# Attention and linear attention on one core: idle matmuls ahead of the second scores, projections planned by their users, products that wait for V's copies

## The chip, the cores and the metric

The kernel runs on one core of one Trainium2 chip. The metric is the device time of one execution in microseconds (us). The core has a matrix engine (PE, whose weight loads are listed apart as PEld), a vector engine (DVE), a scalar engine (ACT), a general engine (POOL), and queues of DMA that are fed by SP and ACT. Each engine works through its own instructions in the order in which the program lists them; semaphores make one wait for another.

## The reference

Two layers on separate inputs of 2048 rows by 512 columns, bf16, 32 heads of 16; their outputs lie side by side.

```python
# layer A: softmax attention
qkv = (x @ wqkv).reshape(B, S, 3, H, Dh)          # S = 2048, H = 32, Dh = 16
p = softmax(einsum("bhqd,bhkd->bhqk", q, k) * Dh ** -0.5)
a = einsum("bhqk,bhkd->bhqd", p, v).reshape(B, S, D) @ wo
# layer B: linear attention with learned feature maps
phi = concat(softmax(x_head @ w_phi), softmax(-(x_head @ w_phi)))   # for q and for k
o = (phi_q @ (phi_k.T @ v)) / (phi_q @ sum(phi_k) + 1e-6)
b = o.reshape(B, S, D) @ wo
return concat([a, b], axis=-1)
```

## The kernel before

**Layer A.** The 32 heads are eight groups of four; the four heads of a group lie in the four 32-row strips of the PE array. A unit is one group and one chunk of 512 queries: 32 units, chunk by chunk, group by group. A unit has 32 steps. One step (L986) computes the scores of two heads, 128 queries by 512 keys, into two PSUM banks with two matmuls on 32 rows each; the two pairs of banks 0 to 3 alternate between steps. DVE then takes the maximum of each row (L1000, 1024 steps in all). After the last step of a segment (a part of a unit: units 0 and 31 have three segments, the others two) DVE folds the maxima (L1010), POOL splits them in two bf16 parts (L1016 to L1019), and SP transposes them (L1021) and writes them into spare rows of QT (L1023). The scores are then computed a second time, transposed and with the maximum subtracted by those rows ("blocks", L1055), ACT takes the exponential (L1062) into a ring of 15 tiles, and "products" (L1108) multiply four such tiles by V, with a column of ones for the sums, into bank 7. Blocks of a segment begin `LAGX` = 8 steps after its last step. Behind a unit ACT copies bank 7 out (X), POOL takes reciprocals and multiplies (L1243), and the output projection of layer A follows by chunks.

**Projections.** `proj(kind, a, c)` makes a job of four matmuls and a copy. For groups 0 and 1 the copy goes straight into QT or KT (ACT, L530 and L532). Groups 2 to 7 are projected in pairs, eight heads at a time: ACT copies into `oct_t`, and two DMAs on SP (L519) spread it over two groups of QT or KT. V's jobs (L491) are copied into VP, one for each of 16 tiles of 128 keys.

**Layer B** runs in the same program as jobs in the background: weights are folded with the feature maps (`fold_job`), and 32 feature-map chains `fm(n)` open at step `FM0 + FMSTEP * n`.

**The planner.** The order of instructions on every engine is fixed when the program is built, by a loop that keeps an account (`_Clock`): `ck.pe` and `ck.rows` say where PE stands, `ck.act` where ACT stands, `ck.d[s]` when step s's maximum is done. Its figures: 1.131 for a step, 0.215 for a matmul, 0.445 from issue to result, 0.477 for an exponential. `tau` is the number of the next step. A job carries a step at which it opens (`slot`), a step at which it is due (`by`), and sometimes a condition (`when`). Once a job is due it goes ahead of the scores; else it is placed only where it fits ahead of the next ones. `XA` holds the account's times at which the four chunks of x may be used. `qt_ready`, `kt_ready` and `vp_ready` say that a projection has been issued; `ready_at` says at what time of the account its result is there, and the scores (`m1_from`) wait for it. `ready_at` is set for groups 0 and 1 only.

Among the fillers, `row_fill` (L1192) and `go_fill` (L1207) place matmuls on zeros where PE would rest, from step `LAG` = 22 on (14 steps of the first segment plus 8). Eleven such matmuls (L562) open the program, ahead of the first two projections.

Group 2's jobs open at steps 36, 42, 48, 54 (keys) and 60 (queries), each due ten steps later:

```python
        at = 36
        for g in range(2, NG, 2):
            for t in group(g):
                add_job(at, *proj(*t), by=at + 10)
                at += 6
```

`group(g)` lists four chunks of keys and then the queries of chunk 0. Unit 2 (group 2, chunk 0) begins at step 64, unit 4 at step 128, unit 6 at step 192.

Of the kernel before, what the change touches and what calls it, by code (L numbers as in the profile page):

```python
# [152 lines left out]
def bass_concat_heads__softmax_full_mha__linear_kernel_hedgehog__prompt_kernel(  # L153
# [9 lines left out]
    NKC = S // 512  # L163
# [16 lines left out]
    COLD = 7.0  # L180
    WARM = 7.4
    TOP = 12.0
    FM0 = 152
    FMSTEP = 25
    units = [(g, c) for c in range(NQC) for g in range(NG)]

    segs = []
# [22 lines left out]
    LAG = seg_end[0] + LAGX  # L210

    with contextlib.ExitStack() as es:
# [165 lines left out]
        def add_job(slot, pieces, fin, by=None, when=None, bank=None):  # L378
            by = slot + BY if by is None else by
            njobs[0] += 1  # L380
            jobs.append((by, slot, njobs[0], pieces, fin, when, bank))
# [106 lines left out]
        def proj(kind, a, c):  # L488
            if kind == "v":
                kt = a  # L490
                pieces = mm_pieces(lambda e, b, ct: e.matmul(  # L491
                    PS[:, b, :], xAT[:, ct, kt * 128:(kt + 1) * 128], wA[:, ct, 1024:1536],
                    start=(ct == 0), stop=(ct == 3)), [t_xa[kt // 4], t_wa[1024]])

                def fin(b, tok, tau):
                    last_proj["v"] = tok
                    vp_ready[kt] = aevac(VP[:, kt, :, 0:16], PS[:, b, :].rearrange("p (h d) -> p h d", d=16),
                                         [tok, t_vp1])
                    return vp_ready[kt]
                return pieces, fin  # L500
            g = a
            wpad = WQp if kind == "q" else WKp
            at = g if g < 2 else 1 + g // 2
            pieces = mm_pieces(lambda e, b, ct: e.matmul(  # L504
                PS[:, b, :], wpad[:, ct, 128 * at:128 * at + 128], xAT[:, ct, c * 512:(c + 1) * 512],
                start=(ct == 0), stop=(ct == 3)),
                [t_xa[c], (t_wqp if g < 2 else t_wqr) if kind == "q" else (t_wkp if g < 2 else t_wkr)])

            def fin(b, tok, tau):
                last_proj[kind] = tok  # L510
                sl = slice(c * 512, (c + 1) * 512)
                if g >= 2:

                    i = n_oct[0] % 2
                    n_oct[0] += 1
                    t = aevac(oct_t[:, i, :], PS[:, b, :], [tok, oct_d.get(i)])
                    dst, dep = (QT, t_qt0) if kind == "q" else (KT, t_kt1)
                    for gg in range(2):
                        oct_d[i] = P.dma("sp", d_oct[i], lambda e, gg=gg: e.dma_start(  # L519
                            dst[0:128:2, g + gg, sl], oct_t[64 * gg:64 * gg + 64, i, :]), [t, dep[g]])  # L520
                    for gg in range(2):
                        (qt_ready if kind == "q" else kt_ready)[(g + gg, c)] = oct_d[i]
                    return t
                if kind == "q" and g == 0 and c == 0:
                    t = P.op("dve", lambda e: e.tensor_copy(QT[:, g, sl], PS[:, b, :]), [tok])
                elif g == 0 and c == 0:
                    t = P.op("dve", lambda e: e.tensor_scalar(
                        KT[:, g, sl], PS[:, b, :], bias_k[:, 0:1], None, ALU.add), [tok, t_bias])
                elif kind == "q":
                    t = aevac(QT[:, g, sl], PS[:, b, :], [tok])  # L530
                else:
                    t = act_op(0.57, lambda e: e.activation(  # L532
                        KT[:, g, sl], PS[:, b, :], ACT.Identity, bias=bias_k[:, 0:1]), [tok, t_bias])
                (qt_ready if kind == "q" else kt_ready)[(g, c)] = t
                ready_at[(kind, g, c)] = ck.act + 0.25
                return t
            return pieces, fin

        def group(g):
            return [("k", g, c) for c in range(NKC)] + [("q", g, 0)]  # L540


        XA = (6.0, 11.9, 14.2, 18.8)
        need = [(4, "k", 0, 1), (6, "k", 0, 2), (8, "k", 0, 3)]
        need += [(LAG + 2 + kt, "v", kt, 0) for kt in range(NKT)]
        need += [(32 + 2 * c, "k", 1, c) for c in range(NKC)] + [(31, "q", 1, 0)]
        for at, t in enumerate(sorted(need)):
            c = t[2] // 4 if t[1] == "v" else t[3]
            add_job(at, *proj(*t[1:]), by=t[0] - 4, when=lambda c=c, v=t[1] == "v": ck.pe > max(XA[c], 11.8 * v))
        at = 36  # L550
        for g in range(2, NG, 2):
            for t in group(g):
                add_job(at, *proj(*t), by=at + 10)
                at += 6
        at = 170
        for c in range(1, NQC):
            for g in (0, 1, 2, 4, 6):
# [61 lines left out]
        def fold_job(x, ct):  # L619
            piece = mm_piece(4, cols=128, fn=lambda e, b, t: e.matmul(  # L620
                PS[:, b, t * 128:(t + 1) * 128], wT[4 * x + t][:, ct * 128:(ct + 1) * 128], BD[:, t, :],
                start=True, stop=True), deps=lambda: [BL["wt"], BL["bd"]])

            def fin(b, tok, tau):
                wf_pe[(x, ct)] = tok
                wf_tok[(x, ct)] = aevac(Wf[:, x, ct, :], PS[:, b, :], [tok, last_proj["k"]])
                return wf_tok[(x, ct)]
            return [piece], fin

        for i in range(8):  # L630
            add_job(125 + 3 * i, *fold_job(1 - i // 4, i % 4), by=130 + 3 * i)

        kv_last = {}

# [435 lines left out]
        def pv_at():  # L1070
            n = npv[0]
            if n == len(of_pv) or nblk[0] < min(pv_blk[0] + BATCH, len(of_b)):
                return None
            v = of_pv[n]
            per = 4 // segs[v][2]
            if any((n - seg_pv[v]) * per + j not in vp_ready for j in range(per)):
                return None
            at = max(exp_end[B] for B in range(pv_blk[0], min(pv_blk[0] + BATCH, len(of_b))))
            if n == seg_pv[v] and segs[v][1] == 0 and v > 0:
                if segs[v][0] - 1 not in xev_end:  # L1080
                    return None
                at = max(at, xev_end[segs[v][0] - 1])
            return ck.full("col", at)
# [117 lines left out]
        def go_fill():  # L1201
# [4 lines left out]
            for cq in range(4):  # L1206
# [3 lines left out]
                    skip_group_check=(bank == 7)),  # L1210
                    [t_zmv, t_ones, dep] if cq == 0 else [], signal=False)

        def emit_xev(u):
            ub = u % 2
            deps = [pv_t[u]]
            if u >= 1:
                deps.append(mul_t[u - 1])
            xev_t[u] = aevac(X[:, :], PVB, deps)
            xev_end[u] = ck.act + 0.18

            pv_open[0] = True
            pv_free[:] = [xev_end[u], xev_t[u]]
            lr_t[u] = P.dma("sp", d_lr[ub], lambda e: e.dma_start(lr[:, ub, :], X[16:128:32, :]),
                            [xev_t[u], lb_t.get(u - 2)])
# [90 lines left out]
        def step(tau):  # L1315
# [14 lines left out]
            for v in rm_in_slot.get(tau, []):  # L1330
                emit_mchain(v)
                ck.extra += 0.11

        tau = 0
        while tau < total_q1 or npv[0] < len(of_pv) or jobs or running or calls:
            bg_read(tau, ck.act + 0.05 if nblk[0] else 1e9)
# [29 lines left out]
            if due - HARD < first < 1e8 and tau < total_q1 and (second is None or second > first - 0.25):  # L1366
                step(tau)
                tau += 1
                if tau > LAG:
                    row_fill(tau)  # L1370
            elif cold and ck.full("col", fill_place()[1]) < min(soon, pick[0] if pick else 1e9) + 0.1:
                go_fill()
            elif pick is not None and pick[0] <= soon + 0.02:
                if pick[1] == 1 and not in_hand():
                    ck.begun = tau
                pick[2](tau)
            elif (tau >= LAG and ck.work(ck.pe) < WARM
                  and ck.full("col", fill_place()[1]) + 0.213 <= min(soon, pick[0] if pick else 1e9)):
                go_fill()
            elif pick is not None and pick[0] < soon + 0.1 and pick[1] == 0:  # L1380
                pick[2](tau)
            elif second is not None and second <= first + 0.05 and not (first <= feed and first < second):
                block_go(tau)
                if tau >= LAG:
                    row_fill(tau)
            elif running and not running[0][0] and running[0][4] <= first + 0.1:
                bg_read(tau, 1e9)
            elif first > 1e8:
                ck.pe = max(ck.pe + 0.2, max(ck.rows))
            else:  # L1390
                step(tau)
                tau += 1
                if tau > LAG:
                    row_fill(tau)
# [55 lines left out]
```

## Time and profile before

| | |
|---|---|
| median of 3 runs | 1264.46 us (1263.28 to 1265.48) |
| profiled execution | 1259.73 us, its span 1257.9 us |
| busy in the span | PE 1171.4, PEld 470.0, DVE 1205.4, ACT 1161.9, POOL 631.8 us |
| DVE L1000, maxima | 1024 instructions, 1171.7 us busy, 13.2 us idle before them |
| ACT L1062, exponentials | 2048 instructions, 1057.8 us busy, 62.6 us idle before them |
| first maximum starts, last folding of maxima | 10.27 us, 1222.87 us |
| chain that ended last | ACT 44%, DVE 30%, PE 21% of the span |

Times within the profile are microseconds from the start of the span. A line of the timeline gives start, length (of the merged run of instructions), engine, source line, operation, output and input, and the count; in brackets stands how long the engine was idle before it and what it then waited for. "PEclk" and "granted clock" are the PE clock as a share of full speed.

### The profile page before, as it was taken

The numbers are of one execution on the slowest core, as the hardware profiler recorded it, in microseconds if no ns is written. First come the engines' busy times: TensorE is split into PE (matmuls) and PEld (weight loads), VectorE is DVE, ScalarE is ACT, GpSimd is POOL, SyncE is SP. The second block draws the span as 40 slices with busy tenths as digits, with TensorE's granted clock in tenths as the row PEclk, the third lists the DMA queues.
The fourth block names the chain that finished last, engine by engine and source line by source line (L and its number), as shares of the span: only waits on it lengthen the run. The fifth ranks groups of instructions, "written<-read, shape, count | busy, mean of one in ns | idle before, by whom it ended". The sixth has DMA issues, their size and how long they took to land.

```text
span 1257.9 us, 37296 instructions
## 1 busy us (share of the span) xinstructions
PE 1171.4 (93%) x16122; PEld 470.0 (37%) x16230; DVE 1205.4 (96%) x1229; ACT 1161.9 (92%) x2296; POOL 631.8 (50%) x724
## 2 busy tenths in 40 slices
PE   7989999999999999999999999999999999999998
PEld 2333343333333333333333334333333333333334
DVE  6989999999999999999999999999999999999980
ACT  2788999999999899999999899999999999999997
POOL 3301111363558266666558355556757555658520
PEclk8999999999999999999999999999999999999999
DMA  6123411011100111011001112212121112121211
GB/s 134 38 49 67 63 12 9 5 12 12 13 7 13 21 13 12 7 14 13 9 8 9 26 9 25 30 16 38 17 33 18 43 24 34 9 37 21 35 17 28
DMA packets 84253, 31.46 MB, mean 25 GB/s; under 512 B 71864, under 2 KB 82104, under 8 KB 84088
## 3 DMA queue, kind: packets, MB, share of 16 engines
q1 hardware_dynamic: 82216, 28.02, 15.7%
q8 instruction: 127, 2.08, 0.7%
q10 hardware_dynamic: 1872, 1.05, 0.3%
q14 instruction: 38, 0.31, 0.1%
HBM read 3.16 MB, written 4.19 MB: 6 GB/s over the span
## 4 chain that ended last, share of the span: by engine, by line
ACT 44%; DVE 30%; PE 21%; POOL 2%; issue 2%; DMA 1%; ACTq 0%; SPq 0%
ACT pT L1062 39%; DVE part L1000 28%; PE PS L1055 5%; PE PS L986 4%; PE PS L504 2%; PE PS L1207 2%; PE PS L1108 2%; PE PS L1192 2%; ACT eB L696 1%; PE PS L491 1%; POOL den_t L856 1%; PE PS L650 1%; PE PS L880 1%; ACT oct_t L464 1%; ACT X L464 1%
## 5 line engine op out<-in xcount | busy, mean ns | idle before, releaser
L1000 DVE TENSOR_REDUCE part<-PS 128x2 f32<-128x1024 f32 x1024 | 1171.7, 1218 | 13.2 <-PE PS L1192 5.5
L1062 ACT ACTIVATE pT<-PS 128x512 bf16<-128x512 f32 x2048 | 1057.8, 639 | 62.6 <-PE PS L986 23.7
L1055 PE MATMUL PS<-QT,KT 32*128 32x256 bf16 (+1 forms) x4224 | 669.1, 269 | 21.6 <-ACT pT L1062 2.7
L1192 PE MATMUL PS<-zmv,ones_t 32*128 32x512 bf16 x1755 | 589.5, 383 | 0.1
L986 PE MATMUL PS<-KT,QT 32*128 32x512 bf16 x2048 | 447.3, 385 | 19.9 <-DVE part L1000 11.4
L1055 PEld LDWEIGHTS PS<-QT,KT 32*128 32x128 bf16 x4224 | 228.8, 92 | 368.1 <-ACT pT L1062 217.2
L1016 POOL TENSOR_SCALAR stage<-mrow 128x8 bf16<-128x8 f32 (+1 forms) x66 | 15.7, 238 | 406.0 <-DVE mrow L1010 406.0
L1108 PE MATMUL PS<-pT,VP 128*17 128x256 bf16 (+1 forms) x4224 | 203.3, 272 | 10.5 <-ACT pT L1062 1.6
L986 PEld LDWEIGHTS PS<-KT,QT 32*128 32x128 bf16 x2048 | 116.2, 91 | 115.0 <-DVE part L1000 73.8
L1192 PEld LDWEIGHTS PS<-zmv,ones_t 32*128 32x128 bf16 x1755 | 146.5, 91 | 1.4 <-PE PS L1055 0.7
L1207 PE MATMUL PS<-zmv,ones_t 128*17 128x256 bf16 x2880 | 141.4, 276 | 1.4
L1108 PEld LDWEIGHTS PS<-pT,VP 128*17 128x17 bf16 x4224 | 61.5, 88 | 120.0 <-ACT pT L1062 57.4
L1228 POOL TENSOR_TENSOR lr<-lr,neg 128x16 f32<-128x16 f32 x31 | 90.6, 2922 | 22.9 <-DMA lr<-X 11.9
L1243 POOL TENSOR_TENSOR QT<-X,Yd 128x256 bf16<-128x256 f32 x62 | 43.8, 727 | 91.0 <-DMA Yd<-Yd 91.0
L856 POOL TENSOR_TENSOR den_t<-den_t,neg 128x32 f32<-128x32 f32 x16 | 87.1, 5446 | 1.3
L727 POOL TENSOR_TENSOR wB<-wB,neg 128x32 f32<-128x32 f32 x16 | 87.0, 5437 | 0.0
L1207 PEld LDWEIGHTS PS<-zmv,ones_t 128*17 128x17 bf16 x2880 | 55.6, 89 | 75.0 <-issue 66.0
L747 POOL TENSOR_TENSOR wA<-eB,rB 128x512 bf16<-128x512 bf16 x64 | 66.9, 1069 | 0.2
L688 POOL TENSOR_TENSOR uB<-pB,mB 128x512 f32<-128x512 bf16 x32 | 33.6, 1049 | 33.0 <-DVE mB L672 33.0
L704 POOL TENSOR_TENSOR sB<-eB 128x512 f32<-128x512 bf16 x32 | 36.9, 1154 | 5.2 <-ACT eB L696 5.2
L707 POOL TENSOR_TENSOR sB<-sB 128x256 f32<-128x256 f32 x64 | 36.2, 566 | 5.0
L650 PE MATMUL PS<-WKp,xBT 128*128 128x512 bf16 x99 | 31.2, 383 | 7.3 <-ACT pT L1062 6.1
(90 smaller groups left out, 568.1 us busy)
## 6 DMA issues: line engine op xcount, KB each, us to landing
Yd<-Yd SPq DMA_DIRECT2D x124, 32.0 KB, 3.2
out_dram<-xAT SPq DMA_DIRECT2D x16, 128.0 KB, 1.8
KT<-oct_t SPq DMA_DIRECT2D x24, 64.0 KB, 2.1
QT<-oct_t SPq DMA_DIRECT2D x24, 64.0 KB, 2.0
out_dram<-OA SPq DMA_DIRECT2D x12, 128.0 KB, 1.7
mcols<-stage SPq DMA_TRANSPOSE x66, 2.2
QT<-mcols SPq DMA_DIRECT2D x62, 4.0 KB
wA<-in_A_wqkv_dram SPq DMA_DIRECT2D x2, 384.0 KB, 4.6
```

The source lines that it names most:

```text
L727: t = P.op("pool", lambda e: e.tensor_tensor(wB[:, n % 4, :], wB[:, n % 4, :], neg1[:, 0:1].broadcast_to([128, 32]), ALU.pow), [cx["r"], t ...
L747: t = P.op("pool", lambda e, a=a: e.tensor_tensor(f4[:, :, a, :], e4[:, :, a, :], r2[:, :, 1 - a].unsqueeze(2).broadcast_to([128, H, 16]), ...
L856: cx["rd"] = P.op("pool", lambda e: e.tensor_tensor(den_t[:, :], den_t[:, :], neg1[:, 0:1].broadcast_to([128, 32]), ALU.pow), [t, t_neg])
L986: tok = P.op("pe", lambda e, r=r, bank=2 * (q1 % 2) + i: e.matmul(PS[:, bank, :], QT[32 * r:32 * r + 32, g, q0:q0 + 128], KT[32 * r:32 * r ...
L1000: r1[q1] = P.op("dve", lambda e: e.tensor_reduce(part[:, u % 2, 2 * pr:2 * pr + 2, qt, kc], PS[:, b:b + 2, :], AX.X, ALU.max), deps)
L1055: m2_t[B] = P.op("pe", lambda e, j=j: e.matmul(PS[:, bank, j * w:j * w + w], KT[32 * r:32 * r + 32, g, (kt + j) * 128:(kt + j + 1) * 128], ...
L1062: exp_t[B] = P.op("act", lambda e: e.activation(pT[:, slot, :], PS[:, bank, :], ACT.Exp, scale=0.25), [m2_t[B], slot_reader.get(slot)])
L1108: tok = P.op("pe", lambda e, B=B, r=r, j=j: e.matmul(PVB[32 * r:32 * r + 17, lo:lo + w], VP[:, kt + j, 4 * g + r, :], pT[:, B % RING, j * ...
L1192: fill_tok[0] = P.op("pe", lambda e: e.matmul(PS[:, 7, :], ones_t[32 * r:32 * r + 32, :], zmv[32 * r:32 * r + 32, :], start=False, stop=Fa ...
L1207: P.op("pe", lambda e, cq=cq: e.matmul(PS[32 * cq:32 * cq + 17, bank, 0:256], ones_t[:, 0:17], zmv[:, 0:256], start=(bank != 7), stop=(ban ...
L1228: rec = P.op("pool", lambda e: e.tensor_tensor(lr[:, ub, :], lr[:, ub, :], neg1[:, 0:1].broadcast_to([128, 16]), ALU.pow), [lr_t[u], t_neg])
L1243: mul_t[u] = P.op("pool", lambda e, sl=sl, lo=lo: e.tensor_tensor(QT[:, g, lo:lo + 256], X[:, sl], Yd[:, sl], ALU.mult), [sh_t[u], xev_t[u ...
```

## The change

A new function `go_warm` issues one full-array matmul of zeros into bank 7. The planner's loop calls it before step `LAG` and before the first block, where such a matmul would end ahead of the next scores, of the next job that can go, and of the next chunk of x in `XA`. `XA` gets slightly earlier times. The five projections of each pair of groups (2, 4, 6) put the queries first, have a list of opening steps of their own, and are due six steps later instead of ten; those of group 1 get deadlines by the step of their first use. `ready_at` is now set for V's copies too, where a product must wait for it in the account, and, with 6.0 us for the DMA, for groups 2 to 7. The last product of a unit is not planned before the multiply of the unit before it. The folds of layer B open five steps later; its feature maps begin at 156 with a spacing of 24.5 steps (before: 152 and 25).

```diff
-    FM0 = 152
-    FMSTEP = 25
+    FM0 = 156
+    FMSTEP = 24.5
...
+                    ready_at[("v", kt)] = ck.act + 0.25
                     return vp_ready[kt]
...
                         (qt_ready if kind == "q" else kt_ready)[(g + gg, c)] = oct_d[i]
+                        ready_at[(kind, g + gg, c)] = ck.act + 6.0
...
-        XA = (6.0, 11.9, 14.2, 18.8)
+        XA = (6.0, 11.4, 14.0, 18.6)
         need = [(4, "k", 0, 1), (6, "k", 0, 2), (8, "k", 0, 3)]
         need += [(LAG + 2 + kt, "v", kt, 0) for kt in range(NKT)]
-        need += [(32 + 2 * c, "k", 1, c) for c in range(NKC)] + [(31, "q", 1, 0)]
+        need += [(30 + 8 * c, "k", 1, c) for c in range(NKC)] + [(29, "q", 1, 0)]
...
-        at = 36
+        OCT = [42, 46, 51, 56, 62, 68, 73, 78, 83, 88, 94, 100, 106, 112, 118]
         for g in range(2, NG, 2):
-            for t in group(g):
-                add_job(at, *proj(*t), by=at + 10)
-                at += 6
+            for i, t in enumerate(group(g)[-1:] + group(g)[:-1]):
+                at = OCT[5 * (g // 2 - 1) + i]
+                add_job(at, *proj(*t), by=at + 6)
...
-            add_job(125 + 3 * i, *fold_job(1 - i // 4, i % 4), by=130 + 3 * i)
+            add_job(130 + 3 * i, *fold_job(1 - i // 4, i % 4), by=134 + 3 * i)
...
+            if n + 1 == len(of_pv) or segs[of_pv[n + 1]][0] != segs[v][0]:
+                if segs[v][0] > 0 and segs[v][0] - 1 not in mul_t:
+                    return None
             at = max(exp_end[B] for B in range(pv_blk[0], min(pv_blk[0] + BATCH, len(of_b))))
+            at = max([at] + [ready_at[("v", (n - seg_pv[v]) * per + j)] for j in range(per)])
...
+        def go_warm():
+            start = ck.full("full", 0.0)
+            ck.run_full("full", start, 0.216)
+            P.op("pe", lambda e: e.matmul(PS[:, 7, :], ones_t[:, :], zmv[:, :], start=True, stop=True),
+                 [t_zmv, t_ones], signal=False)
...
+        def ready_x():
+            return min((x for x in XA if x > ck.pe), default=1e9)
...
+            elif tau < LAG and not nblk[0] and ck.full("full", 0.0) + 0.316 < min(
+                    due - 0.1, pick[0] if pick else 1e9, ready_x()):
+                go_warm()
```

In the list of needs, a job is due four steps before the first number of its tuple.

## The prediction

> **What bounds the kernel now.** I read the page first, for busy shares and the clock by slices.
>
> ```profile
> PE 1171.4 (93%) x16122; PEld 470.0 (37%) x16230; DVE 1205.4 (96%) x1229; ACT 1161.9 (92%) x2296; POOL 631.8 (50%) x724
> ...
> PEclk8999999999999999999999999999999999999999
> ```
>
> DVE, which takes the maximum of every score block (1024 reduces, L1000), is the bound: 52.5 us of the 1257.9 us span are not DVE time. So I asked next where DVE rests. Before the first reduce (10.27) it has some 7 us of rest that the change does not touch, and behind the last one (about 1222.9) the tail has no reduces. In the timeline of DVE the rest lies in two places, 15 to 24 us and 89 to 100 us:
>
> ```profile
> 10.27 4.62 DVE L1000 TENSOR_REDUCE part<-PS 128x2 f32<-128x1024 f32 x4 [0.49 <-PE PS L986]
> 16.41 1.23 DVE L1000 TENSOR_REDUCE part<-PS 128x2 f32<-128x1024 f32 x1 [1.52 <-PE PS L986]
> 18.34 1.23 DVE L1000 TENSOR_REDUCE part<-PS 128x2 f32<-128x1024 f32 x1 [0.71 <-PE PS L986]
> 19.85 1.23 DVE L1000 TENSOR_REDUCE part<-PS 128x2 f32<-128x1024 f32 x1 [0.28 <-PE PS L986]
> 22.21 1.23 DVE L1000 TENSOR_REDUCE part<-PS 128x2 f32<-128x1024 f32 x1 [1.13 <-PE PS L986]
> 23.75 8.17 DVE L1000 TENSOR_REDUCE part<-PS 128x2 f32<-128x1024 f32 x7 [0.32 <-PE PS L986]
> ...
> 92.14 1.23 DVE L1000 TENSOR_REDUCE part<-PS 128x2 f32<-128x1024 f32 x1 [3.24 <-PE PS L1192]
> ...
> 94.78 1.23 DVE L1000 TENSOR_REDUCE part<-PS 128x2 f32<-128x1024 f32 x1 [0.18 <-PE PS L986]
> 97.14 2.58 DVE L1000 TENSOR_REDUCE part<-PS 128x2 f32<-128x1024 f32 x2 [1.14 <-PE PS L1192]
> 99.98 13.81 DVE L1000 TENSOR_REDUCE part<-PS 128x2 f32<-128x1024 f32 x12 [0.26 <-PE PS L986]
> ```
>
> The brackets say for how long DVE waited and for whom: 3.96 us in the head, 4.82 us at step 64. From 100 to 1223 us the gaps of DVE sum to under 4 us. Why does PE come late? The table of stretches, cut where the clock changes (columns: stretch, length, busy time of PE, PEld, DVE, ACT, POOL, granted clock, DMA share, GB/s):
>
> ```profile
> 9.43:12.84 3.41, 0.94 (x8) 0.29 (x8) 2.92 (x4) 0.00 (x0) 2.48 (x2) 1.00 1.19 282
> 12.84:16.26 3.42, 2.64 (x8) 0.54 (x6) 2.04 (x2) 0.69 (x1) 0.00 (x0) 0.50 1.01 275
> 16.26:19.67 3.41, 3.41 (x11) 0.62 (x9) 2.45 (x2) 0.69 (x1) 2.71 (x2) 0.50 1.17 161
> 19.67:23.08 3.41, 3.19 (x10) 0.82 (x9) 2.10 (x2) 0.60 (x1) 2.54 (x6) 0.50 0.49 34
> 23.08:26.50 3.42, 3.42 (x17) 1.02 (x16) 3.04 (x4) 1.35 (x3) 0.00 (x0) 1.00 0.00 0
> 87.94:91.35 3.41, 0.30 (x2) 0.01 (x1) 0.96 (x1) 1.42 (x3) 0.00 (x0) 1.00 0.19 41
> 91.35:94.76 3.41, 3.18 (x28) 1.04 (x28) 2.45 (x3) 1.51 (x3) 1.04 (x4) 0.50 0.00 0
> ```
>
> A thinly used stretch of 3.41 us is followed by clock 0.50: three stretches after 12.84, two after 91.35. At 0.50 PE is busy without a break (3.41 of 3.41) and DVE still waits: PE is the bound there. The second drop has a cause of its own, in the timeline:
>
> ```profile
> 88.90 1.12 SPq L519 DMA_DIRECT2D QT<-oct_t  x2
> 91.49 0.10 PEld L986 LDWEIGHTS PS<-KT,QT 32*128 32x128 bf16 x2 [3.54 <-DMA QT<-oct_t]
> ```
>
> PE, in order, stands before the scores of step 64 because the queries of groups 2 and 3 were issued to DMA only at 88.90.
>
> **Part 1, idle matmuls and the earlier key projection.** I use the planner's account for order alone, never for time. In it steps 0 and 1 go out at 9.85 and step 2 at 11.49. Between them nothing is ready, so the new branch places a matmul of 0.216 while its start plus 0.316 stays under XA[1] = 11.4: five (10.17, 10.38, 10.60, 10.81, 11.03). Step 2 then carries the account past 11.4, where 11.9 was wanted before, so the four matmuls of keys chunk 1, and one of V, now stand before step 3 instead of behind it. Chunk 1's DMA landed at 8.54 and V's weights at 11.78, so neither should wait.
>
> Does the clock hold? Count a 128-row matmul of 512 columns as 1 and a 32-row score tile as 1/4. The stretch 9.43 to 12.84 held 8 tiles, 2 units, and the clock fell; at the half clock about 6.5 units (16.26 to 19.67) did not bring it back and about 7.5 (19.67 to 23.08) did. The new order puts 1 + 5 + 0.5 + 4 + 1 = 11.5 into the first stretch, 9.5 if its edges shift to the worst place, and about 11 into the next. I take: it holds.
>
> At the full clock, keys chunk 1 start 0.32 behind step 2's scores (as 23.32 to 23.64), their copy 1.07 later (23.64 to 24.71) for 0.69: 11.55 + 2.08 = 13.63, before the score buffer of step 4 comes free (10.27 + 3 x 1.135 + 0.09 = 13.76; 1.135 is the pace of reduces without a gap, 18.26 us per 16 with their row maximum). So DVE runs on without a gap. Fifteen reduces then take 14 x 1.135 + 1.22 = 17.1 and end at 27.4; they ended at 31.92. Gain 4.5; the other way, 3.96 of gaps plus 5 x 0.085 of overlap lost by a lone reduce (1.22 against 1.135) is 4.4. **Minus 4.4**, bounds 0 (the clock falls all the same) and 4.5. The five idle matmuls cost 5 x 0.216 = 1.08 us of PE (0.216 is the pace of the four at 8.02: 1.03 less 0.379 for the last, by 3) inside its 1.32 us wait for step 0's reduce: nothing. Without that cover step 2 is late by up to 1.1. Exponentials start later (38.96) and hang on the same steps, so they move along.
>
> The Trainium skill, page "TensorE: Matmul & The Clock Gate", section "HAM oscillation — how this bites in real kernels", gives as the rule that PE must have no idle gap over about 3.4 us. By it alone the clock should not have fallen at 12.84, since the longest gap there was 1.32 us, and five fillers would change nothing: the sum would be Part 2 alone. The row contradicts it.
>
> **Part 2, order of the eight-head projections.** Before, group 2's queries came last, opened at step 60 and due by 70, though their user is step 64. Now they come first, opened at 42 and due by 48, 16 steps or 18 us ahead. What the chain needs is 85.58 (first matmul of it) to 91.49 (scores run), 5.9 us. Keys of chunk 3 come last, at 62 due by 68, for step 88: 20 steps left. Groups 4 and 6 were never late (due by 124 at the latest, users 128 and 192) and stay so. Each projection still issues 4 matmuls, one copy and two DMAs on SP, past the same transposes of row maxima (L1021, 1.1 us each); rows must be cleared by POOL first (last clearing 57.2, group 2's by 38.8). Gain: 4.82 of gaps plus 4 x 0.085 of lost overlap = 5.16. **Minus 5.2**, bounds 0 (another late operand takes its place) and 5.2.
>
> Keys of group 1 are now planned by user (due by 26 + 8c rather than 28 + 2c), so V's projections go ahead of them; same work, covered by DVE, which was 10.00 of 10 us busy at 30 to 50. More deadlines are tight (6 steps of slack rather than 10), and a job that is due goes ahead of scores: price in the rivals.
>
> **Part 3, products.** A product now waits in the account until V's copy is done, so PE stands less before L1108. Behind it stand only PE's next scores. DVE's gap of 0.72 at 60.36 is the nearest row: between minus 0.7 and plus 0.7, I take 0. The extra condition on the last product of a unit (previous unit's multiply emitted) is met 32 steps after by a step planned some 14 to 20 steps after: 0.
>
> **Part 4, fold and feature maps.** The last map moves from step 927 to 915.5, so linear attention's last copy (0.59 at 1227.28, in the tail where ACT is the chain) can fall under the reduces: 0 to minus 0.6. ACT's load grows 2% in that part alone; it is 94 to 98% busy per 100 us. I take 0. The tail is set by structure: the last two segments' blocks may start only 8 steps behind.
>
> **Sum.** -4.4 - 5.2 + 0.1 for slips of the new order (PE must finish step 3's scores within about 0.2 of their need) = -9.5. The profiled execution took 1259.73 with its span of 1257.9; it becomes 1250.2. The median of the runs lies 4.73 higher at 1264.46, and the same saving gives **1255.0**.
>
> **Rivals.** (a) The idle matmuls do not hold the clock (the skill's rule, or late data): only Part 2, 1264.46 - 5.2 = 1259.3. For: the row that raised the clock needed 7.5 units, a narrow basis. Against: 11.5 is far above 2. Chance 0.12. (b) The head is won, but a new late operand stalls PE near step 64: 1264.46 - 4.4 = 1260.1. Against: 12 us to spare. Chance 0.06. (c) Slower: jobs past their due step go ahead of scores. A whole projection is 4 x 0.216 + 0.2 = 1.06 us of PE, while scores have 1.135 - 0.445 - 0.06 = 0.63 of play (0.445 from issue to result, which 0.43 from 9.84 to 10.27 bears out; 0.06 for the buffer's release, the account's figure): 0.43 us of DVE lost each. With 36 projections before step 130, 15.5 us, net +6, 1270.5; it decides from 22 of them paying in full. For: dues are nearer. Against: whole V projections stand between scores at 24 to 38 us without a gap in DVE. Chance 0.08. (d) The gains come and small new gaps or a longer tail eat them: about 1264.5, chance 0.04. That leaves 0.70 for the forecast.
>
> **Numbers.** All of DVE's gaps between first and last reduce with their lost overlap are about 13 us: 1251.5 is the floor, and I put the low end at 1251.8. The high end takes in (a) and (b): 1260.8. What is left out is (c), (d) and odds of the edge, under 2 in 10. A difference under 0.2%, 2.5 us, counts as none. Faster 0.70 + 0.12 + 0.06 = 0.88; same 0.04; slower 0.08.
>
> **What would show it.** Right: clock 1.00 from 9.4 to 100 us, five matmuls of the new line before step 2, reduces of the head in one run that ends near 27.4, no wait for oct_t's DMA before L986, first reduce of unit 2 near 84.5 (88.90, where DVE came free, less 4.4) instead of 92.14, the last reduce near 1213. Wrong: clock 0.50 behind 12.8; gaps of 0.3 to 0.4 us at many reduces from 24 to 130 us; or a tail longer than 35 us behind the last reduce.

## The result, and the profile after

The changed kernel took 1247.68 us (median of four, 1246.6 to 1248.86) against 1264.97 us before; the ratio is 0.9865 (95% interval 0.9848 to 0.9882). I had forecast 1255.0 with a low end of 1251.8: the direction is right, the size is not; the time lies below the range. (The 1264.97 has one execution more than the 1264.46 above.) The profiled execution took 1246.60 us (before 1259.73), its span 1244.7 us. So the profiled pair moved by 13.1 us and the medians by 17.3.

In the program after, the maxima are L1002 (L1000 before), the first scores L988, the blocks L1057, the exponentials L1064, the products L1115, the fillers L1199 and L1214, and the new idle matmuls L1223. The page of the kernel after (busy time by engine; the clock by slices; the group of the maxima with its idle time):

```profile
PE 1165.4 (94%) x16194; PEld 470.6 (38%) x16299; DVE 1203.5 (97%) x1229; ACT 1161.1 (93%) x2296; POOL 630.9 (51%) x724
...
PEclk9999999999999999999999999999999999999999
...
L1002 DVE TENSOR_REDUCE part<-PS 128x2 f32<-128x1024 f32 x1024 | 1169.7, 1214 | 2.5 <-PE PS L988 1.0
```

The maxima waited 2.5 us in all, where they had waited 13.2, and the granted clock of this execution is 1.00. The timeline of DVE after, at the two places shown before:

```profile
8.99 17.20 DVE L1002 TENSOR_REDUCE part<-PS 128x2 f32<-128x1024 f32 x15 [0.49 <-PE PS L988]
26.11 0.16 DVE L1012 TENSOR_REDUCE mrow<-part 128x4 f32<-128x16 f32 x1
...
80.16 3.49 DVE L1002 TENSOR_REDUCE part<-PS 128x2 f32<-128x1024 f32 x3 [0.19 <-PE PS L1199]
83.57 0.17 DVE L1012 TENSOR_REDUCE mrow<-part 128x8 f32<-128x32 f32 x1
83.66 18.30 DVE L1002 TENSOR_REDUCE part<-PS 128x2 f32<-128x1024 f32 x16
```

The first fifteen reduces are one run of 17.20 us, and nothing waits at step 64 (the 83 us here). And the head of the kernel after in stretches of 3.41 us (busy PE, PEld, DVE, ACT, POOL, clock, DMA share, GB/s):

```profile
9.43:12.84 3.41, 3.27 (x16) 0.98 (x15) 3.41 (x4) 0.69 (x1) 1.21 (x2) 1.00 1.22 283
12.84:16.26 3.42, 3.26 (x17) 1.11 (x17) 3.42 (x4) 1.58 (x3) 0.51 (x1) 1.00 0.98 282
```

PE was busy for 0.94 us of the first of these and is busy for 3.27 now. Cut at the foldings of maxima (the L1012 and L1010 lines), the two profiled spans differ as follows:

| stretch | before | after | difference |
|---|---|---|---|
| start to first maximum | 10.27 | 8.99 | -1.28 |
| to the first folding (step 14) | 21.57 | 17.12 | -4.45 |
| to the one at step 48 | 39.84 | 38.99 | -0.85 |
| to the one in the middle of unit 2 (step 80) | 42.02 | 36.78 | -5.24 |
| to the last one | 1109.17 | 1107.15 | -2.02 |
| tail | 35.03 | 35.67 | +0.64 |
| span | 1257.90 | 1244.67 | -13.2 |

The first row is not the change's: the first weights landed earlier, and over the runs below the first maximum started anywhere from 8.99 to 10.28 us with this stage unchanged. The two places that I had costed came out as costed. What I missed must lie in the long middle and in the four microseconds between the profiled pair and the medians.

### The profile page after: what moved, and what is told of

It is laid out like the page before. It is cut to its first block, busy times and chain, and to the rows that moved or that the text cites. A ratio compares the mean times of both kernels' runs of the same rounds, so it can differ in the third digit from the quotient of the medians.

```text
span 1244.7 us, 37448 instructions
## 1 busy us (share of the span) xinstructions
PE 1165.4 (94%) x16194; PEld 470.6 (38%) x16299; DVE 1203.5 (97%) x1229; ACT 1161.1 (93%) x2296; POOL 630.9 (51%) x724
## 4 chain that ended last, share of the span: by engine, by line
ACT 41%; DVE 39%; PE 18%; issue 2%; DMA 0%; POOL 0%; ACTq 0%; SPq 0%; POOLq 0%
DVE part L1002 37%; ACT pT L1064 36%; PE PS L1057 5%; PE PS L988 3%; PE PS L1214 2%; PE PS L1115 2%; PE PS L1199 2%; PE PS L505 1%; ACT eB L698 1%; PE PS L652 1%; ACT oct_t L464 1%; ACT X L464 1%; PE PS L882 1%; ACT pB L464 1%; PE PS L912 1%
## 5 line engine op out<-in xcount | busy, mean ns | idle before, releaser
L1002 DVE TENSOR_REDUCE part<-PS 128x2 f32<-128x1024 f32 x1024 | 1169.7, 1214 | 2.5 <-PE PS L988 1.0
L1064 ACT ACTIVATE pT<-PS 128x512 bf16<-128x512 f32 x2048 | 1058.3, 640 | 56.3 <-PE PS L988 25.6
L1057 PE MATMUL PS<-QT,KT 32*128 32x256 bf16 (+1 forms) x4224 | 669.1, 269 | 20.9 <-ACT pT L1064 2.8
L1199 PE MATMUL PS<-zmv,ones_t 32*128 32x512 bf16 x1695 | 567.3, 382 | 0.0
L988 PE MATMUL PS<-KT,QT 32*128 32x512 bf16 x2048 | 445.3, 383 | 15.0 <-DVE part L1002 10.6
L1057 PEld LDWEIGHTS PS<-QT,KT 32*128 32x128 bf16 x4224 | 227.4, 92 | 366.7 <-ACT pT L1064 217.2
L1115 PE MATMUL PS<-pT,VP 128*17 128x256 bf16 (+1 forms) x4224 | 202.7, 272 | 9.1 <-ACT pT L1064 1.1
L988 PEld LDWEIGHTS PS<-KT,QT 32*128 32x128 bf16 x2048 | 116.6, 91 | 106.9 <-DVE part L1002 73.4
L1214 PE MATMUL PS<-zmv,ones_t 128*17 128x256 bf16 x3000 | 144.2, 275 | 1.3
L1199 PEld LDWEIGHTS PS<-zmv,ones_t 32*128 32x128 bf16 x1695 | 139.7, 91 | 0.2
L1115 PEld LDWEIGHTS PS<-pT,VP 128*17 128x17 bf16 x4224 | 61.9, 88 | 115.4 <-issue 57.3
L1214 PEld LDWEIGHTS PS<-zmv,ones_t 128*17 128x17 bf16 x3000 | 57.4, 89 | 74.4 <-issue 66.0
L690 POOL TENSOR_TENSOR uB<-pB,mB 128x512 f32<-128x512 bf16 x32 | 33.5, 1047 | 35.2 <-DVE mB L674 35.2
```

The source lines that it names most:

```text
L988: tok = P.op("pe", lambda e, r=r, bank=2 * (q1 % 2) + i: e.matmul(PS[:, bank, :], QT[32 * r:32 * r + 32, g, q0:q0 + 128], KT[32 * r:32 * r ...
L1002: r1[q1] = P.op("dve", lambda e: e.tensor_reduce(part[:, u % 2, 2 * pr:2 * pr + 2, qt, kc], PS[:, b:b + 2, :], AX.X, ALU.max), deps)
L1057: m2_t[B] = P.op("pe", lambda e, j=j: e.matmul(PS[:, bank, j * w:j * w + w], KT[32 * r:32 * r + 32, g, (kt + j) * 128:(kt + j + 1) * 128], ...
L1064: exp_t[B] = P.op("act", lambda e: e.activation(pT[:, slot, :], PS[:, bank, :], ACT.Exp, scale=0.25), [m2_t[B], slot_reader.get(slot)])
L1115: tok = P.op("pe", lambda e, B=B, r=r, j=j: e.matmul(PVB[32 * r:32 * r + 17, lo:lo + w], VP[:, kt + j, 4 * g + r, :], pT[:, B % RING, j * ...
L1199: fill_tok[0] = P.op("pe", lambda e: e.matmul(PS[:, 7, :], ones_t[32 * r:32 * r + 32, :], zmv[32 * r:32 * r + 32, :], start=False, stop=Fa ...
```

## Experiments

Two theories stood against my sum (theory A): B, that a wait of PE costs more than itself, since it starts a stretch of half clock of chance length; and C, that the parts which I had put at nothing carry much of the gain.

### One part of the change on the kernel before

b_again is the kernel before. b_warm adds the idle matmuls, the new `XA` and the condition on the last product of a unit. b_oct adds only the new order, steps and dues of the eight-head projections with their `ready_at`. b_both has the idle matmuls, the new `XA` and the projections of b_oct, without the condition on the last product; the products' account, the deadlines of group 1, the folds and the feature maps are as before.

```diff
# b_warm                                   # b_oct
+ def go_warm(): ...                       - at = 36 ... by=at + 10
+ XA = (6.0, 11.4, 14.0, 18.6)             + OCT = [42, 46, ...] ... queries first, by=at + 6
+ elif tau < LAG and ...: go_warm()        + ready_at[(kind, g + gg, c)] = ck.act + 6.0
```

> The kernel before, unchanged, for its spread. Theory A (the 4 us by which the medians moved more than the profiled executions is chance in one profiled execution): spans scatter around 1262 with no link to the granted clock, and the profile shows the same two half-clock stretches, 10.2 us at 12.8 and 6.8 us at 91. Theory B (executions of the kernel before differ in how long the half clock lasts at the head): the granted clock is lower, 0.985 to 0.990, in the executions that take 1264 and more, and 0.993 only in those near 1260.

> The kernel before with the idle matmuls, the new times of x's chunks, and the extra condition on the last product of a unit; the projections' order and dues as before. Theory A: only the head is won, 4.4 us: near 1260.3, with the half clock gone at 12.8 and still there at 91. Theory B: the head's variable loss goes too, 8 to 9 us: near 1256. Theory C (what the rest of the change does to the order is worth more than the idle matmuls): under 3 us.

> The kernel before with the queries first in the eight-head projections, their new list of steps, dues after six steps, and the 6.0 us of DMA in the account; no idle matmuls. Theory A: only the stall at step 64 is won, 5.2 us: near 1259.6; the half clock at 12.8 stays, that at 91 goes. Theory B: the same 5.2 us, and the scatter of the kernel before stays. Theory C: over 7 us.

> The kernel before with the idle matmuls and new times of x's chunks and with the new order of the eight-head projections; deadlines of group 1, products' account, folds and feature maps as before. Theory A and my sum: 9.6 us, near 1255.2. Theory B: 13 to 14 us, near 1251. Theory C: 10 us or less, as the remaining 3 to 7 us come from the parts left out here.

| kernel | median us | executions | ratio (95%) |
|---|---|---|---|
| b_again | 1263.61 | 1260.1 to 1268.0 | 0.9998 (0.9983 to 1.0014) |
| b_warm | 1263.06 | 1262.4 to 1264.3 | 1.0000 (0.9987 to 1.0013) |
| b_oct | 1263.73 | 1260.8 to 1265.3 | 0.9997 (0.9981 to 1.0012) |
| b_both | 1257.30 | 1256.8 to 1258.3 | 0.9950 (0.9930 to 0.9969) |

Theories A and B both missed b_warm, b_oct and b_both: each part alone gains nothing, and both together gain 6 us. Theory C's numbers came in b_warm (under 3 us) and b_both (10 us or less), not in b_oct (over 7 us). In b_again, time and clock go together as theory B said: the executions near 1260 us have a granted clock of 0.992 or 0.993, those above 1264 us one of 0.982 to 0.988. But in its profile the longer half clock lies behind step 64, not at the head, where B had looked for it. The parts do not fail where they act. In b_warm the stretch to the first folding is 17.11 us (4.5 less), in b_oct the one from step 48 to step 80 is 36.76 us (5.3 less), just as costed. The time comes back later. In b_oct, in order of time (timeline, lines of PE and DVE near 1063 us; L834 belongs to linear attention):

```profile
1063.32 0.30 PE L834 MATMUL PS<-kvd,WQp 128*128 128x68 bf16 x4 [2.89 <-DMA WQp<-wA]
...
1067.21 1.23 DVE L1001 TENSOR_REDUCE part<-PS 128x2 f32<-128x1024 f32 x1 [3.52 <-PE PS L987]
```

PE, in order, stood 2.89 us before a matmul of linear attention whose transposed operand had not landed, the scores behind it came late, and DVE waited 3.52 us; the half clock followed for 6.8 us. The tail of b_oct is 39.2 us instead of 35.0: 53 exponentials were left when the last maximum was folded, where 46 were left before; at 0.52 us each (1057.8 us for 2048) that is 3.6 us more for ACT, an estimate that is not the whole rule, as a_oct_old below has 51 left and a tail of 35.2 us. In b_warm the tail is 38.8 us, and linear attention's last copy (into `xAT`) runs 31.7 us behind the last folding, where it had run 4.4 us behind it:

```profile
1254.06 0.60 ACT L464 ACTIVATE xAT<-PS 128x512 bf16<-128x512 f32 x1 [0.27 <-PE PS L880]
```

So shifting the head or the projections moves every later job against layer A. That the old start and spacing of the feature maps then no longer fit is taken up below. Whether the condition on the last product costs b_warm anything was not run by itself.

### One part undone on the changed kernel

```diff
# a_fm_old                        # a_nowarm                             # a_oct_old: old list, dues and order,
- FM0 = 156                       - elif tau < LAG and not nblk[0] ...   #   no ready_at for groups 2 to 7
- FMSTEP = 24.5                   -     go_warm()                        # a_nopv
+ FM0 = 152                       # a_xa_old                             - at = max([at] + [ready_at[("v", ...)] ...
+ FMSTEP = 25                     + XA = (6.0, 11.9, 14.2, 18.8)         # after_again: unchanged
```

> The changed kernel with the feature maps at 152 and every 25 steps, as before the change. Theory C1 (the new start and spacing of the feature maps keep linear attention's chain clear of layer A's, and get its last copies out of the tail): 4 to 9 us slower than the changed kernel, 1252 to 1257, with a late copy of linear attention in the tail and waits of PE behind ACT's copy of bank 7 or behind a DMA of linear attention. My sum (its part worth 0 to 0.6): near 1248.3.

> The changed kernel without the idle matmuls ahead of the second scores, all else kept. My sum: 4.4 us slower, near 1252, with the half clock for about 10 us from 12.8. Theory C2 (any shift of the head re-rolls the order behind it, and the feature maps were fitted to this one order): over 7 us slower, with gaps of DVE behind 100 us.

> The changed kernel with the eight-head projections in the old order (queries last), at the old steps and dues, without the 6.0 us in the account. My sum: 5.2 us slower, near 1253, with PE standing over 3 us before step 64 and the half clock behind it. Theory C2: over 8 us slower.

> The changed kernel with products that do not wait for V's copies in the account. My sum: within 0.7 us of the changed kernel, near 1247.7. Theory C3 (the account keeps PE from standing before a product while V is copied, which holds up scores): 1 to 3 us slower, with gaps of DVE between 30 and 60 us. Theory C2: over 3 us slower with gaps elsewhere.

> The changed kernel with the old times of x's chunks: the idle matmuls stay, but keys of chunk 1 go behind step 3 again. My sum (the idle matmuls hold the clock): the half clock stays away at 12.8, the head is as good within 1.2 us. Theory D (the earlier keys do it, as the run without idle matmuls kept the full clock too): the clock falls at the head and 3 to 5 us are lost, with gaps of DVE from 14 to 24 us.

> The changed kernel, unchanged, for its spread. Theory B: as no stall starts a half clock behind the head, all executions lie within 3 us, 1246.5 to 1249.5, where the kernel before scatters over 9 us. Theory A: a spread like that of the kernel before.

| kernel | median us | executions | ratio (95%) |
|---|---|---|---|
| after_again | 1248.16 | 1247.2 to 1249.7 | 0.9882 (0.9858 to 0.9906) |
| a_fm_old | 1265.75 | 1255.8 to 1272.2 | 1.0010 (0.9975 to 1.0045) |
| a_nowarm | 1250.76 | 1250.2 to 1251.2 | 0.9899 (0.9856 to 0.9942) |
| a_oct_old | 1252.88 | 1250.2 to 1260.3 | 0.9924 (0.9900 to 0.9947) |
| a_nopv | 1251.40 | 1250.0 to 1259.0 | 0.9913 (0.9884 to 0.9943) |
| a_xa_old | 1249.71 | 1248.5 to 1250.9 | 0.9892 (0.9865 to 0.9918) |

The changed kernel again lies within 2.5 us, as theory B said, though six of its ten executions (first ones included) have a granted clock of 0.997 to 0.999: one to two stretches of half clock still come in those. Taking back the two numbers of the feature maps costs the whole gain, more than any theory expected, and the executions scatter over 16 us. Without the idle matmuls the head is as fast as with them (timeline of DVE, a_nowarm). The 2.6 us are lost elsewhere: at 103 us PE stands 2.5 us for ACT's copy into `oct_t`, DVE waits for PE (second line), the half clock comes for 6.83 us, and the stretch from step 80 to step 96 takes 22.4 us instead of 18.2:

```profile
9.76 17.19 DVE L1002 TENSOR_REDUCE part<-PS 128x2 f32<-128x1024 f32 x15 [0.49 <-PE PS L988]
...
104.42 1.23 DVE L1002 TENSOR_REDUCE part<-PS 128x2 f32<-128x1024 f32 x1 [1.88 <-PE PS L1057]
```

With the idle matmuls but the old times of x's chunks, keys of chunk 1 stand behind step 3 again, and the head is worse (timeline of DVE and stretches, a_xa_old):

```profile
9.96 4.62 DVE L1002 TENSOR_REDUCE part<-PS 128x2 f32<-128x1024 f32 x4 [0.49 <-PE PS L988]
14.94 1.23 DVE L1002 TENSOR_REDUCE part<-PS 128x2 f32<-128x1024 f32 x1 [0.36 <-PE PS L988]
16.88 1.23 DVE L1002 TENSOR_REDUCE part<-PS 128x2 f32<-128x1024 f32 x1 [0.71 <-PE PS L988]
18.61 3.49 DVE L1002 TENSOR_REDUCE part<-PS 128x2 f32<-128x1024 f32 x3 [0.50 <-PE PS L988]
```

```profile
11.41:14.82 3.41, 2.11 (x11) 0.59 (x10) 3.17 (x3) 0.69 (x1) 0.20 (x1) 1.00 1.06 239
14.82:18.23 3.41, 3.41 (x12) 0.74 (x10) 2.45 (x2) 0.69 (x1) 1.46 (x1) 0.50 1.12 243
```

The clock falls for one stretch, and fifteen reduces take 19.1 us instead of 17.1. Theory D's mechanism holds, at less than its 3 to 5 us (the median is 1.6 us up): the earlier keys make the head. With the idle matmuls alone the half clock is one stretch long (granted clock 0.999 in three of four executions), and none comes in the fourth (1.000), which took 1248.53 us. In a_oct_old the sum's number came, 1253, but not its reason: at step 64 PE stands 1.7 us and not over 3, DVE waits 1.5, and the rest is half clock, as the next part shows. In a_nopv the stretch from the first folding to step 48 is 40.1 us instead of 39.0, with a gap of 0.87 us at 52.9; so the account of V's copies is worth 1.1 us there. A further 2.9 us lie between step 80 and the last folding, and two of its eight executions, near 1259 us, have a granted clock of 0.989 where most have 1.000.

### A wait with and without the half clock

a_oct_old keeps a late DMA at step 64. a_oct_fill is the same with idle matmuls where PE stands; b_fill does it to the kernel before, with 26 groups.

```diff
 def emit_m1(q1):
+    if q1 == 64:
+        keep = ck.pe, list(ck.rows), ck.mode, list(ck.heat)
+        for _ in range(14):      # 26 in b_fill
+            go_fill()            # four 256-column matmuls on zeros
+        ck.pe, ck.rows, ck.mode, ck.heat = keep
```

> The changed kernel with the old order of the eight-head projections (as a_oct_old), and 14 groups of four idle 256-column matmuls on zeros right ahead of the scores of step 64, where PE stands for a DMA anyway; the planner's account is put back, so nothing else moves. Theory B (a stall costs its own 1.5 to 3 us, and then up to 30 us at the half clock, as long as chance has it, because the plan does not leave PE room to come back): the clock stays at 1.00 behind step 64, the spread closes from 10 us to under 3, the median falls from 1252.9 to 1249.5 to 1250.5. Theory A (the late queries cost the wait itself): no change, 1252 to 1253, or slower by the matmuls.

> The kernel before, with 26 groups of four idle 256-column matmuls right ahead of the scores of step 64, where PE stands 3.3 us for the queries' DMA; the account is put back, so nothing else moves. Theory B: the wait of 3.2 us stays, the half clock behind it goes (the one at the head stays), the gaps of DVE from 93 to 111 us (1.6 to 5.3 us in the two profiles) go: median 2 to 4 us below the kernel before, 1259 to 1261, spread under 5 us. Theory A: no change.

a_oct_fill took 1249.86 us (1249.4 to 1250.5; ratio 0.9893, 0.9872 to 0.9915): 3.0 below a_oct_old, and the spread fell from 10 us to 1. b_fill took 1257.90 us (1256.1 to 1259.9, and one at 1267.8; ratio 0.9959, 0.9937 to 0.9981): 4.2 below the kernel before. Stretches of a_oct_old around its wait, and the wait of DVE in its timeline:

```profile
80.13:83.54 3.41, 1.60 (x14) 0.59 (x10) 2.30 (x3) 3.11 (x7) 0.00 (x0) 1.00 0.19 41
83.54:114.26 30.72, 30.72 (x260) 8.89 (x258) 20.75 (x20) 18.63 (x35) 4.96 (x6) 0.50 0.25 41
```

```profile
83.96 1.23 DVE L1001 TENSOR_REDUCE part<-PS 128x2 f32<-128x1024 f32 x1 [1.53 <-PE PS L987]
```

and the same stretches of a_oct_fill, with its idle matmuls and the wait in the timeline:

```profile
80.13:83.54 3.41, 3.18 (x72) 1.87 (x72) 2.54 (x3) 3.35 (x7) 0.00 (x0) 1.00 0.18 39
83.54:114.26 30.72, 29.53 (x394) 11.76 (x384) 29.83 (x29) 27.67 (x55) 5.65 (x9) 1.00 0.40 69
```

```profile
82.06 1.71 PE L1218 MATMUL PS<-zmv,ones_t 128*17 128x256 bf16 x56
...
84.13 1.23 DVE L1006 TENSOR_REDUCE part<-PS 128x2 f32<-128x1024 f32 x1 [1.47 <-PE PS L992]
```

The wait of DVE is nearly the same in both, 1.53 and 1.47 us. Behind it DVE worked 20.75 us of 30.72 in the one and 29.83 in the other: the half clock of this execution, one of the two longest of ten, cost 9.1 us, six times the wait. PE was busy through all of it. For the kernel before, two executions of the same program differ in the same way. In b_again the half clock behind step 64 lasts 20.48 us, in the one on which I built my sum it had lasted 6.83:

```profile
89.38:109.86 20.48, 18.26 (x151) 5.20 (x151) 13.05 (x12) 11.91 (x23) 4.95 (x6) 0.50 0.34 48
```

while b_fill, with its wait of 3.04 us, has none there:

```profile
87.94:91.35 3.41, 3.03 (x99) 2.19 (x87) 0.37 (x2) 0.63 (x3) 0.00 (x0) 1.00 0.21 46
91.35:98.18 6.83, 6.45 (x93) 2.84 (x94) 6.83 (x8) 6.78 (x14) 3.56 (x4) 1.00 0.08 17
```

Theory B holds, but for the spread of b_fill: its execution at 1267.8 us has a granted clock of 0.982, so a long half clock can still start elsewhere.

The price can be read from more than these pairs. The kernel before ran 89 more times beside these experiments. A granted clock of c, averaged over a span, means half clock for 2 x (1 - c) of it. So counted, these executions had 18 to 58 us of half clock and spans of 1257.1 to 1269.6 us, and the two go together (correlation 0.98) at 1.0 us of span for each 3.41 us of half clock. That they go together does not say which causes which; the two runs with idle matmuls do.

### The feature maps: better in themselves, or fitted?

a_fm_old_2 is a_fm_old once more; a_fm154 and a_fm158 set `FM0` to 154 and 158 in the changed kernel; b_both_fm is b_both with 156 and 24.5.

> The changed kernel with the old feature maps once more, for another profile: its executions lay between 1255.8 and 1272.2, and the one profiled was the fastest. Theory B: a slower execution shows the same first waits (PE for a DMA of linear attention near 745 us) and a longer stretch of half clock, about 2 us of time lost for each further 3.41 us of it. Theory C1 alone (linear attention collides with layer A): the same clock, and longer waits for DMA.

> The kernel before with idle matmuls, new times of x's chunks, new order of eight-head projections (b_both, 1257.3) and the new start and spacing of the feature maps (156, 24.5); deadlines of group 1, products' account and folds as before. Theory C1 (the new feature maps are better in themselves): 1248 to 1251. Theory C2 (they are fitted to the one order of the whole change): within 3 us of 1257, with waits of PE for linear attention at other places.

> The changed kernel with feature maps two steps earlier (154, every 24.5). Theory C2: somewhere from 1248 to 1262, with a wait of PE behind linear attention that the changed kernel lacks, and a spread over 4 us if it starts the half clock. Theory C1: within 1 us of the changed kernel, 1247 to 1249.

> The changed kernel with feature maps two steps later (158, every 24.5). Theory C2: somewhere from 1248 to 1262, not the same as two steps earlier. Theory C1: within 1 us of the changed kernel, 1247 to 1249.

| kernel | FM0, FMSTEP | median us | executions | ratio (95%) |
|---|---|---|---|---|
| b_both_fm | 156, 24.5 | 1250.48 | 1249.9 to 1251.6 | 0.9898 (0.9872 to 0.9925) |
| a_fm154 | 154, 24.5 | 1260.35 | 1259.1 to 1265.0 | 0.9980 (0.9962 to 0.9999) |
| a_fm158 | 158, 24.5 | 1254.83 | 1252.0 to 1260.5 | 0.9941 (0.9920 to 0.9961) |

a_fm_old_2 took 1271.82 us, and its profile shows the half clock for 12 stretches behind 748 us and for five more at 652 and 1062, where a_fm_old's, at 1255.76 us, shows two behind 745 and no others (stretches of a_fm_old_2, then of a_fm_old):

```profile
744.57:747.98 3.41, 1.85 (x28) 0.78 (x25) 2.48 (x3) 2.51 (x6) 1.41 (x2) 1.00 0.99 162
747.98:788.94 40.96, 40.71 (x422) 13.05 (x422) 30.06 (x33) 30.43 (x58) 19.59 (x19) 0.50 0.10 10
```

```profile
742.01:745.42 3.41, 2.03 (x24) 0.63 (x22) 3.15 (x3) 2.58 (x6) 1.16 (x2) 1.00 1.03 146
745.42:752.25 6.83, 6.79 (x76) 2.39 (x76) 4.47 (x7) 4.28 (x9) 0.25 (x1) 0.50 0.10 17
```

The trigger is the same: PE stands 1.8 and 1.7 us before a matmul of linear attention (L835) for a transposing DMA. In the long stretch DVE lost 40.96 - 30.06 = 10.9 us, 0.9 per 3.41 us, half of what I had expected. At about 1 us each, the 15 stretches more make the 16 us between the two executions. In a_fm154 the same kind of wait falls at 981 us and is longer (waits from 978 to 993 us):

```profile
DVE part L1002 <- PE PS L1057: 5.1, 1, 5.1
PEld PS L835 <- DMA WQp<-wA: 4.1, 1, 4.1
```

Two steps either way cost 12 and 7 us, so 156 is not a good value by itself but one at which linear attention's operands land in time in this order: theory C2 in the main (its 1248 to 1262 us was wide enough to be hit easily). On b_both the same numbers won 6.8 us (1257.30 to 1250.48), as C1 had said. Of the 7.3 us between the two profiled spans, 4.5 lie in the tail: 39.2 us with 56 exponentials left in b_both, 34.7 with 46 left in b_both_fm. The edits of b_both and of the changed kernel differ only in the deadlines of group 1, the products' account and condition, and the folds, and the new maps were not run on the unchanged kernel before, so C1 and C2 are not told apart fully.

## Why the prediction was right or wrong

**The bound and the two places: right.** DVE's gaps were the lever, and each gave in the profiled pair what the sum said: head 4.45 us (I had 4.4), step 64 5.24 us (5.2), first reduce behind step 64 without a wait. The tail, 35.67 us, is over the 35 that I had named as a sign of being wrong; it was 35.03 before, so that sign said little.

**Part 1: right size, wrong cause.** I gave five idle matmuls between steps 1 and 2; there are three, two of them ahead of step 1 (it was not due yet, which I had passed over), and six more stand between 16 and 32 us. The head keeps its full clock without them (the profiled execution of a_nowarm) and loses it with them where keys of chunk 1 stay behind step 3 (a_xa_old, three executions of four). The step that failed is the credit to the fillers in "I take: it holds". With the earlier keys alone, a_nowarm's stretch from 10.37 to 13.78 us (its edges counted back from its fall at 102.53 us) holds 9.5 of the units that I counted in, more than any stretch behind which the clock fell (6.6 at most). That the size came right for another reason than mine is luck.

**Part 2: the term was mis-sized.** I took 4.82 us of gaps plus overlap from one execution, in which the half clock behind the wait was the shortest in any profile (6.83 us; 20.48 in b_again), and carried "the same saving" over to the median. Only 4 of the 89 other executions of that kernel were faster. b_fill puts the price of that half clock at 4.2 us of the median by itself, with the wait still there. The profile of one execution gave the wait; it could not give what the wait set off. That is also why the medians moved by four microseconds more than the profiled pair, together with the draw of the first executions: the median of the 89 is 1262.75 us, that of all ten of the changed kernel 1247.68, 15.1 us less.

**Part 4: the step that failed most.** "0 to minus 0.6" for start and spacing of the feature maps: undone alone, they cost 17.6 us (1248.16 to 1265.75), as the matmuls of linear attention then stand in PE's queue for DMAs that have not landed, the clock falls, and the tail is 38.4 us. What I had costed did not come: the last copy of linear attention still runs in the tail, 2.9 us behind the last folding (4.4 before). I had costed the maps' work, which does not change, and not where their waits fall in PE's order. Gaps of under 4 us from 100 to 1223 us in the kernel before suggest that its own maps fitted its own order (this was not run), and I read them as a property of the stage. With Part 4 at nothing my sum gave 1255.0 us for a_fm_old as well, which took 1265.75: the gains of this part cover a loss that I had not seen, so that the forecast is only 7 us off is in part luck.

**The sum as a sum.** b_warm and b_oct show that the two main terms do not add to the time of a kernel unless the later order holds: each alone was worth at most 0.3 us of the median. Likewise "the tail is set by structure" fails in b_oct, b_warm and b_both, by about 4 us. **Part 3** was put at 0 with 0.7 either way; undone it costs 3.2 us (a_nopv), for 1.1 of which the place is the one that I had looked at.

**The rivals.** None came with its price. The premise of (a) did: the idle matmuls alone did not hold the clock in three executions of four (a_xa_old), but the keys do. Near was also (b), another late operand in place of the removed one; it is what happens in b_oct, a_fm_old and a_fm154, late in the program rather than near step 64. Forced projections (c) cost nothing that the profile after shows: DVE has no gap over 0.2 us between its first maximum and 140 us.

## What to carry to other kernels

A wait of an in-order PE is to be priced with what it does to the clock: its own length, plus, in this kernel where DVE is the bound, about 1 us for each 3.41 us of half clock behind it, and that stretch varies from one execution to the next. So read the granted clock and the spread over several executions before costing a stall from one profile. Where a wait could not be removed, idle matmuls placed in it held the clock behind it and made the wait no longer, in both kernels tried (1.47 us against 1.53, 3.04 against 3.24); and where an order is fixed ahead by an account, numbers that place other work (here `FM0`) are part of any change to it, and have to be set again before a part is judged.

## What the runs showed of the hardware

The half clock comes in whole stretches of 3.41 us, and its start lies differently from one run to the next (12.84, 14.29, 12.95 us at the head of the kernel before, b_again and b_oct). I counted PE's work in each stretch from its groups by shape (1 for a matmul of 128 rows that streams 512 columns, 1/4 of that for one on 32 rows or with 17 output columns; a matmul counts in every stretch that it touches; 16 fit at the full clock, at 0.216 us each; a few records are missing). All 23 falls ahead of the program's end, in 14 profiles, came behind a stretch with at most 6.6 units, though PE was busy for up to 3.18 us of it (b_both, 265.56 to 268.97 us). At the half clock only 8 units fit, and stretches with 1.25 to 8.0 did not bring the clock back; those that did held 6.1 to 8.0. The count gives no sharp level (a stretch of 5.75 units at 465.28 us in b_fill kept the full clock), but it shows the trap. This kernel's work, mostly in such parts of the array, keeps the full clock with a median of under 9 units of 16. To leave the half clock it had to fill 6 to 8 of 8, which did not always suffice, and it stayed there for up to 41 us with PE busy 40.71 of 40.96.

The Trainium skill, page "TensorE: Matmul & The Clock Gate", section "Part 1: The HAM clock gate (the "warmup" mystery)", has the clock fall after an idle window of about 3.4 us and rise after a busy one, in windows that run free of the kernel. The length and the free phase agree with these runs. That a window must be idle, and that a busy one suffices, does not: the clock fell behind stretches with PE busy for 1.6 us and more, up to 3.18, and stayed down behind eight fully busy ones in a row (a_oct_old, 30.72 of 30.72 us busy).
